# The softmax norm of the last two blocks placed in the output loop, on one Trainium2 core

## The chip, the cores and the metric

The kernel runs on one core of a Trainium2 chip. A core has five engines that run side by side, each through its own list of instructions in order: TensorE (PE in the profile, with its weight loads as PEld), VectorE (DVE), ScalarE (ACT), GpSimd (POOL) and SyncE (SP), which here issues nearly all DMAs. They wait for one another by semaphores. The metric is the device time of one execution in microseconds; less is better.

## The reference

A long convolution with a gate gives x, and x goes through a soft mixture of experts. Only the second part matters here:

```python
N, D, E, S_per_e, F = (45824, 128, 8, 4, 1024)
logits = x @ phi                                   # 45824 x 32
d = exp(logits - logits.max(0)); d /= d.sum(0) + 1e-09
slot_input = (d.T @ x).reshape(E, S_per_e, D)      # dispatch
slot_out[e] = relu(slot_input[e] @ w1[e]) @ w2[e]  # eight experts, four slots each
c = exp(logits - logits.max(1)); c /= c.sum(1) + 1e-09
out = c @ slot_out                                 # 45824 x 128
```

So there are two softmaxes of the same logits: down the tokens (d, for dispatch) and across the 32 slots (c, for the way back).

## The kernel before

The convolution fills the first 770 us and is not touched. The mixture works on the 45824 tokens as 358 tiles of 128, in 23 blocks of 16 tiles (the last, `L2` = 22, has 6; `L1` = 21 is the one before). Everything is written in program order by hand: `inorder` fixes the order of the instructions on each engine as the lines stand.

The main loop (L768) takes a block at a time. `logits` makes the block's logits in PSUM on PE; `slot_max`, `spread_max` and `running_max` keep the running maximum down the tokens; `exps` makes the exponentials for d on ACT; `scores` turns the logits on DVE so that a token's 32 lie in one partition; `softmax` subtracts a token's maximum (a reduce on DVE, then a subtraction on POOL, L661) and writes into `Cm`; `norm` makes the exponential of that on ACT (L667) and adds up the 32 by halves on POOL (L669 to L673) into `csum`; `turn_weights` turns the exponentials for d; `dispatch` multiplies them with the tokens on PE and `collect` adds the result to `acc`. `invert` (L700) makes the reciprocals of `csum` on DVE for a range of tiles, `scale` (L721) multiplies a block of `Cm` by them on POOL.

The tail (from L789) does the last two blocks, then the experts, then the outputs. `up` (PE, and a ReLU on ACT) makes 512 hidden values of four experts, `turn_hidden` turns them (PE, and four copies on DVE), `down` (64 matmuls of PE for four experts) sums into `po`. From `po` come, through one more matmul, the slot outputs `so` (L875), multiplied by `share` from `denominator`.

The output loop (L904) has 24 steps: `spread(m)` multiplies the turned weights of 16 tiles (4 and 12 in the first two steps) with `so` in four matmuls (L893), copies the four PSUM results into an SBUF buffer, two by DVE and two by ACT (L900), and issues one DMA of up to 1 MB to DRAM (L901). There are seven such buffers. The weights are turned by `turned` (four transposes of PE, a copy of DVE or ACT), five steps ahead of their use; the first five, `early(0)` to `early(4)`, are turned before the loop. From step 2 on, step m uses block m - 1 of `Cm`, so that `scale` must have run on it; `scale` of blocks 4 to 10, of 11 to 20, and of `L1` and `L2` stand in the tail, each group behind its `invert`.

Just ahead of the output loop the order is: `down(1)`, `norm` of `L1` and `L2`, `scale` of blocks 11 to 20, the copy of `po`, `so`, and then `invert(QL, QN)` and `scale` for `L1` and `L2`.

Of the kernel before, what the change touches and what calls it, by code (L numbers as in the profile page):

```python
# [34 lines left out]
QN = TOK // 128  # L35
# [462 lines left out]
class Moe:  # L498
# [71 lines left out]
    def run(self, ctx):  # L570
        _moe(ctx, self)


def _moe(ctx, mo):
# [3 lines left out]
    NBL = len(blocks)  # L578
# [54 lines left out]
    def running_max(i, rd):  # L633
        pm = pmt[:, 0:4]
        inorder(nc.tensor.matmul(pm, lhsT=reps, rhs=rd, start=True, stop=True))
        inorder(nc.vector.tensor_reduce(out=neg[:, i + 1 : i + 2], in_=pm, axis=AX.X, op=ALU.min))
# [12 lines left out]
    def scores(i):  # L649
        n = blocks[i][1]  # L650
        lts[i] = lt = ms.tile([128, NB, NSLOT], F32, tag="lt", name=f"lt_{i}")
        inorder(nc.vector.transpose(lt[:, :n].rearrange("p q s -> p (q s)"),
                            pls[i][:, :n].rearrange("p q t -> p (q t)")))
# [10 lines left out]
    def norm(i):  # L664
        q0, n = blocks[i]
        cv = Cm[:, q0 : q0 + n, :]
        inorder(nc.scalar.activation(cv, cv, AF.Exp))  # L667
        h = ms.tile([128, NB, NSLOT // 2], F32, tag="hs", name=f"hs_{i}")
        inorder(nc.gpsimd.tensor_tensor(out=h[:, :n], in0=cv[:, :, :16], in1=cv[:, :, 16:], op=ALU.add))  # L669
        for k in (8, 4, 2):  # L670
            inorder(nc.gpsimd.tensor_tensor(out=h[:, :n, :k], in0=h[:, :n, :k], in1=h[:, :n, k : 2 * k],  # L671
                                    op=ALU.add))
        inorder(nc.gpsimd.tensor_tensor(out=csum[:, q0 : q0 + n], in0=h[:, :n, 0], in1=h[:, :n, 1],  # L673
                                op=ALU.add))
# [9 lines left out]
    def dispatch(*ids):  # L684
        pa = pp.tile([128, 128], F32, tag="pa", name=f"pa_{ids[0]}")
        both = {i: (xq.pop(i), evs.pop(i)) for i in ids}
        parts = [(*both[i], k) for i in ids for k in range(blocks[i][1])]
        for m, (X, ev, k) in enumerate(parts):
            a = m % 4
            inorder(nc.tensor.matmul(pa[32 * a : 32 * a + 32, :], lhsT=ev[:, k, :], rhs=X[:, k, :],  # L690
                             start=(m < 4), stop=(m >= len(parts) - 4), tile_position=(0, 32 * a)))
        pas[ids[0]] = pa

    def collect(i):
        inorder(nc.vector.scalar_tensor_tensor(out=acc, in0=acc, scalar=fac[:, i : i + 1],
                                       in1=pas.pop(i), op0=ALU.mult, op1=ALU.add))

    QL = blocks[NBL - 2][0]

    def invert(q0, q1):  # L700
        inorder(nc.vector.tensor_scalar_add(csum[:, q0:q1], csum[:, q0:q1], 1e-9))
        inorder(nc.vector.reciprocal(csum[:, q0:q1], csum[:, q0:q1]))
# [4 lines left out]
    def den_sum():  # L707
        inorder(nc.scalar.activation(fin[:, : NBL - 2], neg[:, 1 : NBL - 1], AF.Exp, scale=-1.0,
                             bias=neg[:, NBL - 1 : NBL]))
        inorder(nc.vector.tensor_mul(sums, sums, fin))  # L710
        inorder(nc.vector.tensor_reduce(out=den, in_=sums, axis=AX.X, op=ALU.add))

    def denominator():
        ps = pmt[:, 4:8]
        inorder(nc.tensor.matmul(ps[:, 0:1], lhsT=reps, rhs=den, start=True, stop=True))
        rs = mp.tile([128, 1], F32, tag="rs", name="rs")
        inorder(nc.vector.tensor_scalar_add(rs, ps[:, 0:1], 1e-9))
        inorder(nc.vector.reciprocal(rs, rs))
        return rs

    def scale(i):  # L721
        q0, n = blocks[i]
        cv = Cm[:, q0 : q0 + n, :]
        inorder(nc.gpsimd.tensor_tensor(  # L724
            out=cv, in0=cv, op=ALU.mult,
            in1=csum[:, q0 : q0 + n].unsqueeze(2).to_broadcast([128, n, NSLOT])))
# [23 lines left out]
    def early(m):  # L750
        pt = pp.tile([128, 4, 128], F32, tag="pt", name=f"ct_{m}", bufs=4)
        turned(m, pt, True)

    EARLY = 5
# [12 lines left out]
    L1, L2 = NBL - 2, NBL - 1  # L767
# [26 lines left out]
    inorder(nc.vector.tensor_tensor(out=rm, in0=rm, in1=rm2, op=ALU.min))  # L794
    rd = spread_max(L1, rm)
    early(0)
    early(1)
    dispatch(L1 - 1)
    running_max(L1, rd)
    collect(L1 - 1)  # L800
    inorder(nc.gpsimd.memset(hT, 0.0))
    exps(L1)
    exps(L2, True)
    early(2)
    early(3)
    scores(L1)
    turn_weights(L1)
    scores(L2)
    turn_weights(L2)
    dispatch(L1, L2)  # L810
    collect(L1)
    den_sum()
    fetch(L2)
    pst = pp.tile([128, 512], F32, tag="pt", name="pst", bufs=4)
    inorder(nc.tensor.matmul(pst[:, :NSLOT], lhsT=acc, rhs=reps[:, :NSLOT], start=True, stop=True))
    siT = mp.tile([128, NSLOT], F32, tag="siT", name="siT")
    inorder(nc.vector.tensor_copy(out=siT, in_=pst[:, :NSLOT]))

    FJ = FF // 128
    hr = mo.obuf[0].rearrange("p (e h f) -> p e h f", e=2, h=2)  # L820
# [2 lines left out]
    def up(eg, hf):  # L823
        ph = pp.tile([128, 512], F32, tag="pl", name=f"ph_{eg}_{hf}", bufs=2)
        for a in range(4):
            inorder(nc.tensor.matmul(ph[32 * a : 32 * a + 32, :], lhsT=siT,
                                     rhs=w1t[:, 4 * eg + a, 512 * hf : 512 * hf + 512],
                                     start=True, stop=True, tile_position=(0, 32 * a)))
        inorder(nc.scalar.activation(hr[:, eg, hf], ph, AF.Relu))

    def turn_hidden(eg, hf):
        pt = pp.tile([128, 4, 4, NSLOT], F32, tag="pt", name=f"ht_{eg}_{hf}", bufs=4)
        for j in range(4):
            inorder(nc.tensor.transpose(pt[:, j].rearrange("p a s -> p (a s)"),
                                        hr[:, eg, hf, 128 * j : 128 * j + 128], ident))
        for a in range(4):
            s = 4 * (4 * eg + a)
            inorder(nc.vector.tensor_copy(out=hT[:, eg, 4 * hf : 4 * hf + 4, a, s : s + 4],
                                          in_=pt[:, :, a, s : s + 4]))

    def down(eg):
        for j in range(FJ):
            for a in range(4):
                inorder(nc.tensor.matmul(po[32 * a : 32 * a + 32, :], lhsT=hT[:, eg, j, a, :],
                                         rhs=w2t[4 * eg + a][:, j, :], start=(eg == 0 and j == 0),
                                         stop=(eg == 1 and j == FJ - 1), tile_position=(0, 32 * a)))
# [2 lines left out]
    up(0, 0)  # L849
    up(0, 1)  # L850
    share = denominator()
    invert(blocks[EB][0], QH)
    turn_hidden(0, 0)
    for i in range(EB, NBL // 2):
        scale(i)
    up(1, 0)
    turn_hidden(0, 1)
    up(1, 1)
    for i in (L1, L2):
        softmax(i)  # L860
    early(4)
    turn_hidden(1, 0)
    down(0)
    invert(QH, QL)
    turn_hidden(1, 1)
    down(1)
    for i in (L1, L2):
        norm(i)
    for i in range(NBL // 2, L1):
        scale(i)  # L870
    inorder(nc.vector.tensor_copy(out=sop, in_=po))
    pr = pp.tile([128, 128], F32, tag="pa", name="pr")
    inorder(nc.tensor.matmul(pr, lhsT=reps, rhs=sop, start=True, stop=True))
    so = mp.tile([128, 128], F32, tag="so", name="so")
    inorder(nc.vector.tensor_scalar_mul(so, pr, share))  # L875
    invert(QL, QN)
    scale(L1)
    scale(L2)
    pps.close()
    pc = ctx.enter_context(tc.tile_pool(name="pc", bufs=1, space=bass.MemoryType.PSUM,  # L880
                                        reuse_waits="tile"))
# [3 lines left out]
    def spread(m):  # L885
        q0, n = starts[m], sizes[m]
        ct = cts.pop(m)
        ot = obs[m % (XB + OB)].rearrange("p (k a t) -> p k a t", a=4, t=128)
        pos = []
        for a in range(min(4, n)):  # L890
            na = (n - a + 3) // 4
            po = pc.tile([128, 4, 128], F32, tag="po", name=f"pw_{m}_{a}", bufs=6)
            inorder(nc.tensor.matmul(po[:, :na].rearrange("p k t -> p (k t)"),  # L893
                             lhsT=so[NSLOT * a : NSLOT * a + NSLOT],
                             rhs=ct[NSLOT * a : NSLOT * a + NSLOT, :na].rearrange("p k t -> p (k t)"),
                             start=True, stop=True, tile_position=(NSLOT * a, 0)))
            pos.append((a, na, po))
        for a, na, po in pos:
            copy = nc.scalar.copy if a % 2 else nc.vector.tensor_copy
            inorder(copy(out=ot[:, :na, a], in_=po[:, :na]))  # L900
        nc.sync.dma_start(out=out[:, 128 * q0 : 128 * (q0 + n)],  # L901
                          in_=ot.rearrange("p k a t -> p (k a t)")[:, : 128 * n])

    for m in range(len(sizes)):  # L904
        spread(m)
        if m + EARLY < len(sizes):
            pt = pc.tile([128, 4, 128], F32, tag="ct", name=f"ct_{m + EARLY}", bufs=2)
            turned(m + EARLY, pt, False)
# [144 lines left out]
```

## Time and profile before

| what | us |
| --- | --- |
| median of 3 runs | 956.37 |
| lowest, highest | 954.85, 958.70 |
| the profiled execution | 951.48 |
| its span, first to last instruction | 949.7 |

| engine | busy us | share of the span |
| --- | --- | --- |
| PE | 902.1 | 95% |
| DVE | 735.0 | 77% |
| ACT | 445.6 | 47% |
| POOL | 382.0 | 40% |

Times in the profile are microseconds from the start of the span. The shares are an average over stages that have different limits; the stage in question is the last 85 us. There, "L701" names line 701 of the kernel as printed above, a tile is called by the program's name for it or for the memory that it lies in (`xreg` holds `acc`, `hT` and the output buffers, `E` holds `Cm` and `csum`, `pw` are the PSUM results of an output step, `ct` and `cs` the turned weights in PSUM and SBUF). In a timeline row stand start, duration, engine, line, operation, output and inputs, shape and count, and in brackets the idle time in front and what ended it.

### The profile page before, as it was taken

Reading aid. Unit: us, or ns where it says so; the run is one execution under the profiler, and the core shown is the slowest. Engines: PE = TensorE matmul, PEld = TensorE weight load, DVE = VectorE, ACT = ScalarE, POOL = GpSimd, SP = SyncE. Lnnn points to the kernel's source line nnn. Section 1 sums busy time; section 2 is a strip of 40 time slices with the busy share of each in tenths; the row PEclk is TensorE's granted clock in tenths of the full one; section 3 lists DMA queues with packets and bytes.
Section 4 is the critical chain, followed back from the end, with each engine's and each line's share of the span. In section 5 each row is a group of like instructions: output and inputs, shape, how many; then the busy total and the mean of one; then the engine's idle time right before and its main releaser. Section 6 shows DMA issues by size and latency. Waiting matters only on the chain.

```text
span 949.7 us, 33000 instructions
## 1 busy us (share of the span) xinstructions
PE 902.1 (95%) x14040; PEld 813.7 (86%) x14040; DVE 735.0 (77%) x1282; ACT 445.6 (47%) x964; POOL 382.0 (40%) x582
## 2 busy tenths in 40 slices
PE   6999999999999999999999999999999989998792
PEld 5999989999999999999999999999999977765341
DVE  7936769698889879879988997998694268876571
ACT  0655447415711741571174157117414458884461
POOL 5002760382076038207603820760282017876700
PEclk9999999999999999999999999999999999999895
DMA  8923985468745745774574577457247798764498
GB/s 258 397 73 123 338 283 174 125 175 248 225 122 183 235 124 173 245 232 121 176 242 123 174 242 223 131 174 245 82 128 241 229 356 270 262 222 109 201 416 373
DMA packets 104239, 201.18 MB, mean 212 GB/s; under 512 B 14167, under 2 KB 65577, under 8 KB 100252
## 3 DMA queue, kind: packets, MB, share of 16 engines
q1 hardware_dynamic: 103806, 198.89, 64.4%
q8 instruction: 111, 1.82, 0.8%
q14 instruction: 36, 0.29, 0.1%
q10 hardware_dynamic: 254, 0.11, 0.0%
q0 software_dynamic: 32, 0.07, 0.0%
HBM read 139.12 MB, written 59.90 MB: 210 GB/s over the span
## 4 chain that ended last, share of the span: by engine, by line
PE 80%; POOL 7%; DMA 4%; DVE 3%; issue 2%; ACT 2%; DVEq 0%; ACTq 0%; SPq 0%
PE p L296 22%; PE p L279 19%; PE p L331 17%; PE p L138 10%; PE f L160 3%; PE f L170 2%; PE pw L893 2%; POOL hs L671 2%; POOL E L661 2%; PE fl L181 2%; DMA out_dram<-xreg 2%; DMA hs<-E 2%; POOL hs L669 1%; POOL E L724 1%; PE ct L738 1%
## 5 line engine op out<-in xcount | busy, mean ns | idle before, releaser
L287 POOL TENSOR_TENSOR T<-m 111x256 f32<-111x256 f32 (+1 forms) x200 | 147.8, 739 | 420.2 <-DVE m L282 420.2
L282 DVE TENSOR_TENSOR m<-p,T 111x1024 f32<-111x1024 f32 (+1 forms) x175 | 200.1, 1207 | 23.9 <-PE p L279 22.9
L296 PE MATMUL p<-tab,T 111*99 111x112 f32 x2048 | 210.5, 261 | 2.6 <-DVE E L356 1.6
L296 PEld LDWEIGHTS p<-tab,T 111*99 111x99 f32 x2048 | 200.2, 170 | 10.2 <-issue 2.7
L279 PE MATMUL p<-T,W 128*111 128x128 f32 x1584 | 194.7, 278 | 0.0
L279 PEld LDWEIGHTS p<-T,W 128*111 128x111 f32 x1584 | 183.0, 173 | 7.3
L340 ACT ACTIVATE vc<-p 128x416 f32<-128x416 f32 x112 | 51.9, 515 | 284.1 <-DVE p L345 192.5
L331 PE MATMUL p<-tab,E 99*64 99x104 f32 x3584 | 172.2, 253 | 2.2 <-ACT E L302 1.1
L331 PEld LDWEIGHTS p<-tab,E 99*64 99x64 f32 x3584 | 161.4, 136 | 10.0 <-issue 1.8
L302 ACT ACTIVATE E<-p 99x448 f32<-99x448 f32 x256 | 130.6, 575 | 82.1 <-PE p L296 82.1
L288 POOL TENSOR_TENSOR T<-m 111x256 f32<-111x256 f32 (+1 forms) x200 | 146.3, 731 | 0.0
L150 ACT ACTIVATE T<-p 128x396 f32<-128x396 f32 x240 | 102.3, 530 | 5.6 <-PE p L138 5.5
L138 PE MATMUL p<-tab1x,x 53*64 53x99 f32 x3776 | 95.7, 248 | 2.3 <-DVE m L282 1.6
L138 PEld LDWEIGHTS p<-tab1x,x 53*64 53x64 f32 x3776 | 84.1, 132 | 9.2 <-DVE m L282 1.8
L345 DVE TENSOR_TENSOR p<-p,vc 128x832 f32<-128x832 f32 x56 | 57.4, 1026 | 14.5 <-ACT vc L340 14.5
L560 ACT ACTIVATE xreg<-pt 128x512 f32<-128x512 f32 x90 | 48.0, 601 | 4.9 <-PE pt L559 3.0
L229 DVE TENSOR_TENSOR x<-x,T 128x448 f32<-128x448 f32 x55 | 34.1, 620 | 18.5 <-DMA x<-in_xf_dram 11.9
L353 DVE TENSOR_TENSOR E<-p,E 128x824 f32<-128x824 f32 x46 | 46.8, 1016 | 1.6
L559 PE MATMUL pt<-ident,xreg 128*128 128x128 f32 x358 | 47.5, 278 | 0.0
L661 POOL TENSOR_TENSOR E<-lt,mx 128x512 f32<-128x512 f32 (+1 forms) x23 | 23.5, 1025 | 59.2 <-ACT et L642 59.2
L559 PEld LDWEIGHTS pt<-ident,xreg 128*128 128x128 f32 x358 | 40.1, 146 | 4.9 <-issue 2.8
L282 DVE TENSOR_TENSOR m<-p,E 111x1024 f32<-111x1024 f32 (+1 forms) x25 | 29.0, 1209 | 18.0 <-ACT E L186 15.4
(108 smaller groups left out, 972.0 us busy)
## 6 DMA issues: line engine op xcount, KB each, us to landing
x<-in_xf_dram SPq DMA_DIRECT2D x118, 256.0 KB, 4.2
out_dram<-xreg SPq DMA_DIRECT2D x21, 1024.0 KB, 12.7
E<-in_xi_dram SPq DMA_DIRECT2D x46, 412.0 KB, 3.9
scr<-E SPq DMA_DIRECT2D x84, 206.0 KB, 3.2
T<-in_vf_dram SPq DMA_DIRECT2D x65, 224.0 KB, 4.9
hs<-E SPq DMA_DIRECT2D x12, 1024.0 KB, 5.1
T<-hs SPq DMA_DIRECT2D x63, 176.0 KB, 3.7
mv<-in_vf_dram SPq DMA_DIRECT2D x42, 224.0 KB, 5.3
```

The source lines that it names most:

```text
L138: steady(g, nc.tensor.matmul(ps[h][RP * d : RP * d + RP, i, s, :], lhsT=sd[js, i, s, d, :], rhs=tab1x[js, J * (s + d) : J * (s + d + 1)], ...
L150: steady(g, nc.scalar.activation(dst, src, AF.Copy))
L279: steady(g, nc.tensor.matmul(ps[:, i].rearrange("p b c -> p (b c)"), lhsT=W[:, k0 + i, :], rhs=Tf[:, :, k0 + i, :], start=True, stop=True))
L282: inorder(nc.vector.tensor_mul(m[:, :n].rearrange("p k s e c i -> p k s (e c i)").rearrange("p k s (b c) -> p k s b c", c=CG), ps[:, :n].u ...
L287: inorder(nc.gpsimd.tensor_tensor(out=Ty[:, 0], in0=m[:, :n, 0, 0], in1=m[:, :n, 1, 1], op=ALU.subtract))
L288: inorder(nc.gpsimd.tensor_tensor(out=Ty[:, 1], in0=m[:, :n, 1, 0], in1=m[:, :n, 0, 1], op=ALU.add))
L296: inorder(nc.tensor.matmul(pk[:, i, 2 * s : 2 * s + 2, :].rearrange("p q r -> p (q r)"), lhsT=T[0:N1, s, 2 * k + i, u // 2, :, u % 2], rhs ...
L302: inorder(nc.scalar.activation(E[:J, :, :, c : c + 2].rearrange("p r q c -> p q r c"), ps[:, k, : 8 * R].rearrange("p (i q r) -> p q r i", ...
L331: inorder(nc.tensor.matmul(pv[RP * h : RP * h + RP, 2 * k + i, w, :], lhsT=E[:J, r, 2 - 2 * w + s, :], rhs=tab4[:, s, o : o + NJ], start=( ...
L340: inorder(nc.scalar.activation(vc[:, w], pv[:, :, 0, :], AF.Copy, scale=2.0 * w - 1.0))
L345: inorder(nc.vector.tensor_tensor(out=pw, in0=pw[:, 1:2].to_broadcast([128, 2, 4, NJ]), in1=vc, op=ALU.add))
L559: inorder(nc.tensor.transpose(pt[:, j, :], self.xt[i][:, k + j, :], self.ident))
```

## The change

- `norm(L1)` and `norm(L2)` move from behind `down(1)` into the output loop, behind `spread(4)`; `invert(QL, QN)` and the two `scale` of `L1` and `L2` move behind `spread(8)`. The ten `scale` of blocks 11 to 20 now stand behind `so`, but POOL, which does nothing between, meets them in the order subtractions of `softmax`, ten `scale`, sums of `norm`.
- `scores(L1)` and `scores(L2)` (the turned logits) move ahead of `exps`; `early(1)` to `early(4)` come in one row behind `exps`; `den_sum` moves behind the copy of `siT`.
- The experts' stage: `turn_hidden(0, 0)` comes ahead of `up(1, 0)` and both first turns ahead of `invert(blocks[EB][0], QH)`; `turn_hidden(1, 0)` comes ahead of the two `softmax`; `down(0)` is done in two halves with `turn_hidden(1, 1)` between, and `invert(QH, QL)` behind that.

No instruction is added or taken away.

```diff
     early(0)
-    early(1)
     dispatch(L1 - 1)
+    scores(L1)
     running_max(L1, rd)
     collect(L1 - 1)
+    scores(L2)
     inorder(nc.gpsimd.memset(hT, 0.0))
     exps(L1)
     exps(L2, True)
-    early(2)
-    early(3)
-    scores(L1)
+    for m in range(1, EARLY):
+        early(m)
     turn_weights(L1)
-    scores(L2)
     turn_weights(L2)
     dispatch(L1, L2)
     collect(L1)
-    den_sum()
     fetch(L2)
...
     inorder(nc.vector.tensor_copy(out=siT, in_=pst[:, :NSLOT]))
+    den_sum()
...
-    def down(eg):
-        for j in range(FJ):
+    def down(eg, j0=0, j1=FJ):
+        for j in range(j0, j1):
...
     share = denominator()
+    turn_hidden(0, 0)
+    up(1, 0)
+    turn_hidden(0, 1)
     invert(blocks[EB][0], QH)
-    turn_hidden(0, 0)
     for i in range(EB, NBL // 2):
         scale(i)
-    up(1, 0)
-    turn_hidden(0, 1)
     up(1, 1)
+    turn_hidden(1, 0)
     for i in (L1, L2):
         softmax(i)
-    early(4)
-    turn_hidden(1, 0)
-    down(0)
+    down(0, 0, FJ // 2)
+    turn_hidden(1, 1)
+    down(0, FJ // 2)
     invert(QH, QL)
-    turn_hidden(1, 1)
     down(1)
-    for i in (L1, L2):
-        norm(i)
-    for i in range(NBL // 2, L1):
-        scale(i)
     inorder(nc.vector.tensor_copy(out=sop, in_=po))
...
     inorder(nc.vector.tensor_scalar_mul(so, pr, share))
-    invert(QL, QN)
-    scale(L1)
-    scale(L2)
+    for i in range(NBL // 2, L1):
+        scale(i)
...
     for m in range(len(sizes)):
         spread(m)
+        if m == 4:
+            for i in (L1, L2):
+                norm(i)
+        elif m == 8:
+            invert(QL, QN)
+            scale(L1)
+            scale(L2)
         if m + EARLY < len(sizes):
```

## The prediction

> **What bounds the kernel now.** I read the chain of waits first, for the tail from the last dispatch on, then the windows over the output loop, and then the timeline between them. The chain, columns start, duration, engine, tile, line:
>
> ```profile
> 872.05 7.15 POOL E L724 x7
> ...
> 879.20 1.01 POOL E L661
> ...
> 884.59 0.21 POOL E L673
> 884.83 1.01 DVE E L701
> ...
> 886.07 0.24 DVE xreg L900
> ...
> 917.75 15.47 DMA out_dram<-xreg
> ```
>
> From 872 to 885 the chain lies on POOL: seven `scale`, then the two `softmax` subtractions, then both `norm`. Then DVE's `invert(QL, QN)` (L701), and only behind it DVE's first copy of an output (L900, 886.07). At the end it is the output DMAs. The windows (columns: window, length, busy of PE, PEld, DVE, ACT, POOL, granted clock, DMA share, GB/s) say how much of the loop is theirs:
>
> ```profile
> 887.00:887.50 0.50, 0.50 (x4) 0.00 (x0) 0.50 (x2) 0.00 (x0) 0.50 (x1) 0.50 0.14 53
> ...
> 889.50:890.00 0.50, 0.50 (x6) 0.00 (x0) 0.00 (x0) 0.17 (x1) 0.50 (x2) 0.50 1.09 455
> ...
> 891.50:892.00 0.50, 0.50 (x7) 0.31 (x5) 0.50 (x2) 0.50 (x2) 0.50 (x2) 0.80 0.01 0
> ...
> 893.00:893.50 0.50, 0.50 (x8) 0.39 (x4) 0.44 (x1) 0.40 (x1) 0.50 (x1) 1.00 0.59 246
> ...
> 905.00:910.00 5.00, 5.00 (x38) 2.41 (x36) 4.26 (x8) 4.00 (x8) 0.00 (x0) 1.00 1.00 413
> ...
> 947.00:947.50 0.50, 0.00 (x0) 0.00 (x0) 0.00 (x0) 0.00 (x0) 0.00 (x0) 0.50 0.20 78
> ```
>
> The first output moves from about 887.4, the second from 889.5, both done by 891.5, and then nothing moves until the third starts at about 893.2. From there the DMA engines are full to about 947.0: 53.8 us for 23.46 MB (128 x 45824 x 4 bytes) less the first two outputs (4 and 12 tiles of 64 KB, 0.26 and 0.79 MB), 22.41 MB, or 0.417 MB/us. The span ends 2.7 us behind. So the end is set by **when the third output can follow the second without a gap**; what follows costs bytes over rate, whatever the engines do, as long as they stay ahead.
>
> **Before the loop, part by part.** What stands on the path to `so` in the timeline:
>
> ```profile
> 862.16 0.22 DVE L629 SCALAR_TENSOR_TENSOR rd<-neg,rm,pmt 128x4 f32<-128x4 f32 x1
> ...
> 862.86 0.16 DVE L636 TENSOR_REDUCE neg<-pmt 128x1 f32<-128x4 f32 x1 [0.48 <-PE pmt L635]
> ...
> 863.20 0.70 ACT L642 ACTIVATE et<-pl,neg 128x512 f32<-128x512 f32 x1
> ...
> 864.09 0.72 DVE L652 STREAM_TRANSPOSE lt<-pl 128x512 f32<-128x512 f32 x1 [0.82 <-ACT et L642]
> ...
> 864.73 0.67 DVE L680 STREAM_TRANSPOSE ev<-et 128x512 f32<-128x512 f32 x1
> ...
> 865.55 1.50 PE L690 MATMUL pa<-xreg,ev 128*32 128x128 f32 x44 [1.80 <-DVE ev L680]
> ...
> 871.12 0.85 DVE L702 RECIPROCAL E<-E 128x112 f32<-128x112 f32 x1
> ...
> 873.58 0.66 PE L738 MATMUL ct<-ident,E 128*128 128x128 f32 x4
> ...
> 875.04 0.23 DVE L701 TENSOR_SCALAR E<-E 128x160 f32<-128x160 f32 x1
> ...
> 875.31 1.15 DVE L702 RECIPROCAL E<-E 128x160 f32<-128x160 f32 x1
> ...
> 877.07 1.96 PE L844 MATMUL pso<-xreg 128*32 128x128 f32 x64
> ...
> 879.97 0.35 DVE L875 TENSOR_SCALAR so<-pr,rs 128x128 f32<-128x128 f32 x1 [0.58 <-PE pr L873]
> ```
>
> *Turned logits first.* `scores(L1)` now stands 0.82 us behind the exponentials on DVE, and `turn_weights(L1)` behind it. Moved up, it runs at 862.4 to 863.1 while DVE had nothing to do but wait for the maximum; it pushes that maximum (862.86, 0.16) by 0.25 us, and the exponentials by as much. `turn_weights` then needs them alone: from 864.2 instead of 864.73, and dispatch from about 865.05, **0.5 us earlier**. Above, the gain could be 0.72 (the whole transpose); below, nothing, if the later maximum eats it.
>
> *early(1) to early(4)* are 15 transposes together; at 0.66 per four 2.5 us of PE, between the maximum (862.8) and the dispatch (865.05), where PE waits 1.80 today. That hides nearly all of them; if not, up to 0.3 is lost. Their ACT copies (about 2.1 us behind the exponentials) are through at 867, before the first `up` has ended and ACT is needed. In return early(4), 0.66 of PE at 873.58, leaves the `down` stretch. `den_sum` behind `siT` costs nothing: `denominator` needs it two microseconds later.
>
> *The FFN order.* `turn_hidden(0, 0)` and `(0, 1)` no longer wait on DVE for `invert(blocks[EB][0], QH)`, 0.85 us with its reciprocal alone; their copies are ready near 871.0 and 872.6. PE's own work, with 0.5 us less in front, 0.66 less for early(4), and `down(0)` in two halves around the last turn, ends `down(1)` at about 878.3 against 879.03: of the 1.16 I leave 0.4 to turns that now follow their ReLU or copy closely and wait for it. DVE has `invert(QH, QL)` (1.15 and 0.23) in front of the copy of `po`; it starts after the last turn's copies, 875.9, and is through near 877.3, one microsecond ahead of its need. So `so` comes **0.7 us earlier**, at 879.6 instead of 880.32. Bounds: 1.3 (dispatch 0.7 and early(4) whole), and 0.4 later (a DVE instruction that is late).
>
> The price is POOL's: its first `scale` starts behind `turn_hidden(0, 1)`, 873.75 instead of 872.05, 1.7 us later. It is off the path now: the loop first needs block 4 (at 880), scaled at 874.8.
>
> **The head of the loop.** The rows that carry it:
>
> ```profile
> 879.16 1.50 POOL L661 TENSOR_TENSOR E<-lt,mx 128x512 f32<-128x512 f32 x2
> ...
> 880.94 0.73 POOL L669 TENSOR_TENSOR hs<-E 128x256 f32<-128x256 f32 x1 [0.27 <-ACT E L667]
> ...
> 881.03 0.41 ACT L900 COPY xreg<-pw 128x128 f32<-128x128 f32 x2
> ...
> 881.39 0.92 PE L893 MATMUL pw<-cs,so 32*128 32x384 f32 x4
> ...
> 884.75 11.57 POOL L724 TENSOR_TENSOR E<-E 128x512 f32<-128x512 f32 x12
> ...
> 884.83 1.00 DVE L701 TENSOR_SCALAR E<-E 128x22 f32<-128x22 f32 x1 [4.51 <-POOL E L673]
> ...
> 886.35 1.65 PE L893 MATMUL pw<-cs,so 32*128 32x384 f32 x4 [4.05 <-DVE xreg L900]
> ...
> 886.55 17.04 SPq L901 DMA_DIRECT2D out_dram<-xreg  x9
> ...
> 888.98 2.09 PE L893 MATMUL pw<-cs,so 32*128 32x512 f32 x8
> ...
> 895.45 1.14 PE L893 MATMUL pw<-cs,so 32*128 32x512 f32 x8
> ...
> 904.77 0.60 ACT L745 COPY cs<-ct 128x512 f32<-128x512 f32 x1
> ...
> 905.42 1.29 DVE L900 COPY xreg<-pw 128x512 f32<-128x512 f32 x2 [0.37 <-PE pw L893]
> ...
> 905.46 1.07 ACT L900 COPY xreg<-pw 128x512 f32<-128x512 f32 x2
> ...
> 906.63 0.68 DVE L745 COPY cs<-ct 128x512 f32<-128x512 f32 x1
> ...
> 908.97 1.29 DVE L900 COPY xreg<-pw 128x512 f32<-128x512 f32 x2 [0.37 <-PE pw L893]
> ```
>
> ACT copied its part of the first output at 881.03; DVE, behind the `invert`, at 886.07. Without it DVE copies beside ACT: **5.0 us gone**. With the 0.7, DVE and ACT are done at about 880.75 and the first DMA is issued at 880.8 instead of 886.55; data followed 0.9 us behind issue.
>
> The ramp shortens too. PE waited over 4 us there, its clock was granted at 0.50 (windows above), and the third output's matmuls took 2.09 us where 1.14 is usual. After the change PE waits for nothing so long. Then with durations from the quoted rows and 0.68 for DVE's ct copy, spread(1) is copied at 882.6, spread(2) at 884.0. The second output's data starts at 883.5 and takes 0.79/0.417 = 1.9 us, to 885.4; the third could start at 884.9. No gap: full from 885.4 with 22.41 MB left, against 893.2 today. That is **7.8 us** in all: 0.7 + 5.0 + 2.1 for the ramp. If the clock dips all the same, the ramp keeps its old shape, and the sum is 5.7.
>
> [...]
>
> **What moves into the loop.** `norm(L1)`, `norm(L2)` behind spread(4): two exponentials on ACT, about 1 us; per two outputs (3.55 us, from 905.42 to 908.97) ACT has four copies of 0.53 and one of 0.60, so it is caught up within two. What they need, POOL's subtractions, is done at 873.75 + 7.15 + 1.5 = 882.4, before spread(4) ends at about 887.6. POOL then has ten `scale` in front of the sums: to 882.4 + 10 x 1.02 (7.15 for seven) = 892.6, and the sums took 3.86 (880.94 to 884.80): **896.5**. `invert(QL, QN)` stands on DVE behind spread(8), copied near 884.0 + 6 x 1.78 = 894.7 (3.55 per two outputs). So DVE waits 1.8 us, plus 0.5 for the two instructions; behind it stand the copies of spread(9) and, through PSUM, PE. By then 0.26 + 0.79 + 7 x 1.05 = 8.4 MB are produced and about 5.3 sent: 3.1 MB, 7.4 us of transfers are waiting. Output 9, late by 2.3 us, still comes some 3 us before DMA runs dry. Cost: nothing. The last blocks are turned at output 17, far behind.
>
> **Rivals.** *The wait returns inside the loop, and costs part.* If POOL ends its sums over 3 us later than 896.5, DMA runs dry, and each further microsecond is lost. For it: POOL starts 1.7 us later and everything piles on it. Against: twelve `scale` took 11.57 us beside DVE's copies of just this loop. With 4.8 us beyond the margin the gain is 3.0: 953.4.
>
> *Head without ramp.* The loop starts early but its first outputs come as slowly as today, because the clock or the order of PSUM buffers holds it: 5.0 to 5.7, 951 us. Against: the second output's matmuls at full clock took 0.92, not 1.65.
>
> *The change doesn't move the end*, if the transfers are slower when started earlier: 956.4. Against: 413 GB/s in the middle, full share, with all engines busy.
>
> *Slower:* the same place, spread(8), with POOL twice as slow. For the whole 7.8 to be eaten, the sums must end after 896.5 + 3.2 + 7.8 = 907.5, and the ten `scale` take 21 us instead of 10.2, 2.1 each. There is one lock-like row that makes this thinkable: L701 on 22 columns took 1.00, from 884.83 to the end of POOL's first `scale`, where 160 columns took 0.23. DVE waited for POOL there, though, not POOL for DVE. [...]
>
> **How the numbers follow.** The profiled execution took 951.48 us (span 949.7), the three runs 954.85 to 958.7, median 956.37; 4.9 us lie between, not seen in the profile. I take the gain off the median: 956.4 - 7.8 = **948.6**. Chances: forecast, gain 5.5 to 10 us, 0.62; head without ramp 0.13; wait in the loop 0.13; no move 0.07; slower 0.05. A measurement of this kernel tells 0.5%, 4.8 us, from no change. So faster 0.75, same 0.20, slower 0.05. The range 944.8 to 953.0 goes from the largest gain (10, and the runs' own spread) to the first two rivals.
>
> **What would show it.** In the new profile: `turn_weights(L1)` right behind the exponentials and dispatch near 865.0; `so` at 879.6; first output issued near 880.8, not 886.5; granted clock 1.00 through the head; DMA full from 883.5 to 939.2 without a gap; a DVE wait of about 2 us for POOL at L701 near 895, with DMA still full beside it. Wrong would be a DMA share under 0.9 between 895 and 905, a `scale` of over 1.5 us, or `so` not earlier than 880.3.

## The result and the profile after

| | before | after |
| --- | --- | --- |
| median of 6 runs, us | 955.89 | 945.38 |
| lowest, highest | 954.00, 958.70 | 942.44, 947.20 |
| profiled execution | 951.48 | 946.41 |
| its span | 949.7 | 944.6 |

The changed kernel takes 0.9896 of the time, 95% interval 0.9873 to 0.992: between 7.6 and 12.1 us less. Forecast were 948.6 us and a gain of 7.8.

The two profiled executions differ by 5.1 us only, and a reader must see why before comparing rows. The change begins behind the exponential of block `L1 - 1` on ACT (L667), the last instruction of the tail that both kernels have at the same point of the same work. From the timelines, before and after:

```profile
862.14 0.63 ACT L667 ACTIVATE E<-E 128x512 f32<-128x512 f32 x1 [1.77 <-POOL E L661]
```

```profile
865.36 0.63 ACT L667 ACTIVATE E<-E 128x512 f32<-128x512 f32 x1 [1.78 <-POOL E L661]
```

Before this **mark** the executions are 3.2 us apart, in code that is the same but for `early(1)`: its turns stand on PE about 1.6 us ahead of the mark in the kernel before, and behind it in the changed one. The mark itself waits for POOL in both (1.77 and 1.78 us). The profile of before is one that was early. From the mark to the end of the span it is 949.7 - 862.14 = 87.6 us before and 944.6 - 865.36 = 79.2 after: **8.3 us less**. I count from the mark from here on.

The chain of waits after the change (start, duration, engine, tile, line):

```profile
876.60 7.16 POOL E L724 x7
883.76 1.47 POOL E L661 x2
885.23 10.06 POOL E L724 x10
...
898.91 0.21 POOL E L673
899.12 0.02 issue
899.15 0.19 DVE E L701
...
915.63 12.56 DMA out_dram<-xreg
```

It still runs through POOL and through the invert (L701), which seems to say that nothing was gained. It only says where it was followed back to: the last copies waited for the buffer of the DMA issued at 915.63, and that issue goes back to the copies behind the invert. That DMA had been full all the while does not show in it. What has changed stands in the timeline of the loop's head:

```profile
881.92 0.35 DVE L870 TENSOR_SCALAR so<-pr,rs 128x128 f32<-128x128 f32 x1 [0.58 <-PE pr L868]
...
882.92 0.49 DVE L894 COPY xreg<-pw 128x128 f32<-128x128 f32 x2 [0.64 <-PE pw L887]
882.95 0.43 ACT L894 COPY xreg<-pw 128x128 f32<-128x128 f32 x2 [6.24 <-PE pw L887]
...
883.47 19.76 SPq L895 DMA_DIRECT2D out_dram<-xreg  x11
...
884.79 1.24 PE L887 MATMUL pw<-cs,so 32*128 32x512 f32 x8
...
899.15 0.18 DVE L701 TENSOR_SCALAR E<-E 128x22 f32<-128x22 f32 x1 [1.26 <-POOL E L673]
```

DVE copies the first output in the same moment as ACT. The first DMA is issued 18.1 us behind the mark, not 24.4. The third output's matmuls take 1.24 us, not 2.09. DVE still waits for POOL's sums, 1.26 us instead of 4.51, at a place where DMA has work. The windows (granted clock, DMA share and GB/s in the last three columns):

```profile
884.25:884.50 0.25, 0.25 (x7) 0.25 (x4) 0.20 (x1) 0.16 (x1) 0.25 (x1) 1.00 0.63 246
...
885.50:886.00 0.50, 0.50 (x7) 0.04 (x1) 0.05 (x1) 0.19 (x1) 0.50 (x1) 1.00 0.00 0
886.00:887.00 1.00, 1.00 (x10) 0.83 (x12) 1.00 (x2) 0.96 (x2) 1.00 (x2) 1.00 0.81 338
...
895.00:900.00 5.00, 5.00 (x32) 2.26 (x31) 3.30 (x7) 4.03 (x8) 3.76 (x12) 1.00 1.01 411
900.00:905.00 5.00, 4.27 (x18) 1.53 (x16) 3.36 (x6) 1.23 (x3) 1.24 (x2) 0.67 1.01 419
...
941.50:942.00 0.50, 0.00 (x0) 0.00 (x0) 0.00 (x0) 0.00 (x0) 0.00 (x0) 0.50 0.71 281
```

DMA is full from about 886.1, the second output, to 941.9. In 900 to 905, behind DVE's late copies, PE's clock drops, to 0.67 on average, and DMA does not notice: 419 GB/s.

### The profile page after: what moved, and what is told of

Same layout as the page of the kernel before. It is cut to its first block, busy times and chain, and to the rows that moved or that the text cites. A ratio compares the mean times of both kernels' runs of the same rounds, so it can differ in the third digit from the quotient of the medians.

```text
span 944.6 us, 32994 instructions
## 1 busy us (share of the span) xinstructions
PE 900.0 (95%) x14040; PEld 813.9 (86%) x14040; DVE 734.7 (78%) x1282; ACT 445.3 (47%) x964; POOL 381.8 (40%) x582
```

## The experiments

Each kernel has a profile of its own, and for each I give the mark, the time from the mark to the end of the span, and the ratio to the kernel before, with its interval.

| kernel | mark | mark to end | ratio |
| --- | --- | --- | --- |
| before | 862.14 | 87.6 | 1 |
| after | 865.36 | 79.2 | 0.9896 (0.9873 to 0.9920) |
| again | 866.58 | 79.1 | 0.9907 (0.9877 to 0.9938) |
| loop_only | 863.09 | 80.5 | 0.9921 (0.9892 to 0.9950) |
| front_only | 865.64 | 88.8 | 0.9997 (0.9977 to 1.0017) |
| wait_early | 864.47 | 92.0 | 1.0029 (1.0011 to 1.0046) |
| warm | 865.77 | 87.3 | 0.9980 (0.9961 to 0.9998) |
| warm_short | 863.95 | 85.2 | 0.9980 (0.9964 to 0.9996) |
| pool_plus4 | 866.83 | 81.9 | 0.9944 (0.9924 to 0.9964) |
| pool_plus10 | 867.72 | 90.0 | 1.0027 (1.0004 to 1.0051) |
| pool_plus10_late | 864.88 | 79.8 | 0.9902 (0.9865 to 0.9939) |
| turn_later | 864.56 | 79.1 | 0.9914 (0.9892 to 0.9936) |
| ffn_back | 864.18 | 79.0 | 0.9893 (0.9860 to 0.9926) |

**again**, the changed kernel unaltered.

> The changed kernel once more, beside new runs of the kernel before. Theory (the gain is 1.3 us of earlier slot outputs, 5.0 us of the wait taken out, and some 2 us of a ramp without a gap, 8.2 us when both profiles are laid on the same instruction, the exponential of block L1-1): ratio about 0.9914 (8.2 us), and in the new profile the DMA ends again about 77 us behind that instruction (84.9 in the kernel before). Rival (about 2 us more are gained somewhere ahead of the tail, since the medians differ by 10.5): ratio 0.989 again, and the instruction that serves as the mark comes earlier than in the kernel before.

From the mark it takes the same as the first time, within 0.12 us, while the marks are 1.2 us apart. The ratio is 0.9907. The rival gets no support from the marks: those of the kernels with the new order in front lie between 864.2 and 867.7, no earlier than those with the old one, 862.1 to 865.8.

**loop_only**, the kernel before with the loop's part alone:

```diff
-    for i in (L1, L2):
-        norm(i)
-    for i in range(NBL // 2, L1):
-        scale(i)
     inorder(nc.vector.tensor_copy(out=sop, in_=po))
...
-    invert(QL, QN)
-    scale(L1)
-    scale(L2)
+    for i in range(NBL // 2, L1):
+        scale(i)
...
         spread(m)
+        if m == 4:
+            for i in (L1, L2):
+                norm(i)
+        elif m == 8:
+            invert(QL, QN)
+            scale(L1)
+            scale(L2)
```

> The kernel before with nothing changed but the place of the norms, of the last invert and of the scales (in and ahead of the output loop, as in the changed kernel). Theory: the wait and the ramp are this part, so 6.5 to 7 us of the 8.2 remain, 949 us, ratio 0.9930; slot outputs 17.8 us behind the mark as before, first output issued at about 19.2, POOL's sums end 1.3 us earlier than in the changed kernel, so that DVE hardly waits in the loop. Rival (the order ahead of the loop brings the gain): under 3 us, ratio over 0.997.

7.1 us of the 8.3 are here. From the timeline of this kernel:

```profile
880.92 0.35 DVE L871 TENSOR_SCALAR so<-pr,rs 128x128 f32<-128x128 f32 x1 [0.58 <-PE pr L869]
...
896.79 0.17 DVE L701 TENSOR_SCALAR E<-E 128x22 f32<-128x22 f32 x1
```

The slot outputs come 17.8 us behind the mark as before, and DVE does not wait at the invert at all, since POOL began its scales earlier than in the changed kernel.

**front_only**, the other half: the changed kernel's order up to the slot outputs, but norms, scales and invert ahead of the loop, where the kernel before has them. The edit is against the changed kernel.

```diff
+    for i in (L1, L2):
+        norm(i)
+    for i in range(NBL // 2, L1):
+        scale(i)
     inorder(nc.vector.tensor_copy(out=sop, in_=po))
...
+    invert(QL, QN)
+    scale(L1)
+    scale(L2)
...
-        if m == 4:
-            for i in (L1, L2):
-                norm(i)
-        elif m == 8:
-            invert(QL, QN)
-            scale(L1)
-            scale(L2)
```

> The changed kernel's order up to the slot outputs, with the norms, the last invert and the scales where the kernel before has them, ahead of the loop. Theory: slot outputs 1.3 us earlier, but POOL starts its scales 1.3 us later and DVE's first copy still waits for POOL's sums, so the first output is issued 1.3 us LATER than before: ratio 1.0014, 957 us, within what can be told from no change and certainly no gain. Rival (the earlier slot outputs are a gain of their own): 1.3 us or more faster, ratio under 0.9986.

```profile
882.21 0.35 DVE L874 TENSOR_SCALAR so<-pr,rs 128x128 f32<-128x128 f32 x1 [0.58 <-PE pr L872]
889.68 1.00 DVE L701 TENSOR_SCALAR E<-E 128x22 f32<-128x22 f32 x1 [7.12 <-POOL E L673]
```

`so` is 1.3 us earlier from the mark (16.6), but DVE now waits 7.12 us for POOL instead of 4.51, and from the mark the kernel takes 1.2 us **more** than before; the ratio cannot be told from 1. The earlier `so` is worth something only with the loop's part.

**wait_early**, the changed kernel with the wait at the wrong place:

```diff
-        if m == 4:
+        if m == 1:
             for i in (L1, L2):
                 norm(i)
-        elif m == 8:
+        elif m == 2:
```

> The changed kernel with the norms behind spread(1) and the last invert and two scales behind spread(2), in place of 4 and 8. POOL's work keeps its order. Theory (the wait for POOL's sums is still there and is only covered by outputs that wait for DMA; at output 2 there are none): DVE waits about 11 us at the invert, DMA runs dry for about 12 us, the third DMA moves at about 12 us later than in the changed kernel; 4 us slower than the kernel before, 960 us, ratio 1.004. Rival (it is enough that the invert stands behind the first outputs): as the changed kernel, ratio 0.990.

```profile
898.23 0.18 DVE L701 TENSOR_SCALAR E<-E 128x22 f32<-128x22 f32 x1 [11.88 <-POOL E L673]
```

```profile
886.00:890.00 4.00, 2.86 (x16) 1.11 (x11) 0.35 (x1) 2.69 (x6) 4.00 (x5) 1.00 0.94 385
890.00:892.00 2.00, 0.00 (x0) 0.00 (x0) 0.00 (x0) 0.00 (x0) 2.00 (x3) 0.68 0.00 0
892.00:896.00 4.00, 0.00 (x0) 0.00 (x0) 0.00 (x0) 0.00 (x0) 3.84 (x6) 0.50 0.00 0
896.00:900.00 4.00, 0.08 (x2) 0.08 (x2) 1.74 (x5) 0.00 (x0) 2.92 (x9) 0.50 0.00 0
```

The same instructions in the same order on POOL, and the kernel is slower than before, by 4.5 us from the mark (by the ratio, 1.1 to 4.4). DMA has sent its three outputs by 890 and then has nothing for over ten microseconds. So the place in the loop is the change; "into the loop" alone would have been a loss.

**pool_plus4, pool_plus10 and pool_plus10_late** measure the cover. In the changed kernel POOL gets extra work ahead of the last sums, 9 memsets in the first and 22 in the other two; in the last alone the invert moves to step 12. The edit shows both, with the first one's count:

```diff
     obs = mo.obuf + mo.xbuf
+    junk = mp.tile([128, 512], F32, tag="junk", name="junk")
...
         if m == 4:
+            for k in range(9):
+                inorder(nc.gpsimd.memset(junk, 0.0))
             for i in (L1, L2):
                 norm(i)
-        elif m == 8:
+        elif m == 12:
```

> The changed kernel with nine extra memsets of 128x512 on POOL (about 4 us) ahead of the sums of the last two norms. Theory (DVE's wait in the loop is covered by outputs that queue for DMA; by the changed kernel's trace output 9 is copied at 902.8 and DMA would run dry about 1.9 us after that): DVE waits about 5.3 us at the invert, DMA is without work for about 2 us, mark to end 81.3 instead of 79.2. Rival (no cover at all: each us of POOL is lost): 83.2. Rival (the cover is larger than 4 us): 79.2.

> As pool_plus4 with 22 memsets, about 10 us. Theory: the same margin of 1.9 us, so 8 us are lost and the whole gain with them: mark to end 87.3, no better than the kernel before (87.6). Rival (no cover): 89.2. Rival (a large cover): under 83.

> As pool_plus10, with the last invert and two scales behind spread(12) instead of spread(8). Theory (the place sets the cover: by then more outputs wait for DMA and POOL's sums are nearly done): DVE waits 4 to 5 us at the invert, DMA stays full, mark to end 79.2 to 79.7, all of the loss is gone though POOL's work is the same. Rival (the extra POOL work costs by itself, wherever the invert stands): 85 or more.

The memsets were longer than I had assumed. From the timelines of pool_plus4 and pool_plus10:

```profile
896.71 5.17 POOL L903 MEMSET junk<- 128x512 f32 x9
...
905.73 0.18 DVE L701 TENSOR_SCALAR E<-E 128x22 f32<-128x22 f32 x1 [6.37 <-POOL E L673]
```

```profile
897.60 12.73 POOL L903 MEMSET junk<- 128x512 f32 x22
...
914.18 0.18 DVE L701 TENSOR_SCALAR E<-E 128x22 f32<-128x22 f32 x1 [13.93 <-POOL E L673]
```

5.17 us on POOL cost 2.7 (81.9 against 79.2), 12.73 cost 10.8: all but 2.5 and 1.9 us is lost, and from the first to the second 7.6 us more of POOL cost 8.1. The loss is not one gap of DMA but two. In pool_plus4:

```profile
907.00:908.00 1.00, 0.58 (x2) 0.50 (x4) 1.00 (x3) 0.00 (x0) 0.82 (x2) 0.50 0.24 98
908.00:909.00 1.00, 1.00 (x4) 0.00 (x0) 0.56 (x1) 0.00 (x0) 0.00 (x0) 0.50 0.33 139
...
914.00:915.00 1.00, 1.00 (x9) 0.13 (x6) 0.00 (x0) 0.28 (x1) 0.00 (x0) 0.89 0.33 139
```

The first gap is the wait. At 413 GB/s it leaves out 1.4 us of transfers, and DVE waits 5.1 us longer than in the changed kernel: the wait alone has a cover of 3.7 us (in pool_plus10, 9.1 us left out and 12.7 waited longer: 3.6). The second gap, 0.85 us from 913 to 915 (1.4 in pool_plus10, with 342 and 367 GB/s in the halves of 920 to 930), comes behind outputs that PE made at the clock of 0.50 that the wait had left it, until about 914.2.

The expected 81.3 and 87.3 become 82.5 and 90.0 with these durations; 81.9 and 90.0 were measured. That they fit is partly luck: the output copied at 902.8 in the changed kernel is output 10, counted from 0 as the steps are. Output 9 was issued at 901.45, so that its margin is 3.3 us and not 1.9, and the clock, which the expectation leaves out, took about the difference back. With the invert four steps later the 12.73 us cost 0.6:

```profile
911.36 0.18 DVE L701 TENSOR_SCALAR E<-E 128x22 f32<-128x22 f32 x1 [6.85 <-POOL E L673]
```

DVE waits 6.85 us, and DMA stays at 401 GB/s or more in each of the windows of a microsecond from 905 to 918. It dips only later, to 380 GB/s in 920 to 925, behind outputs that PE made at a clock of 0.50 (910.2 to 920.4).

**warm and warm_short** ask what the ramp of 2 us was. In the kernel before, PE gets work to do while DVE waits, 26 matmuls in the first and 14 in the second:

```diff
             turned(m + EARLY, pt, False)
+        if m == 0:
+            fill = pc.tile([128, 4, 128], F32, tag="ct", name="fill", bufs=2)
+            for k in range(26):
+                inorder(nc.tensor.matmul(fill[:, k % 4, :], lhsT=reps, rhs=ident, start=True, stop=True))
```

> The kernel before with its wait left as it is, and 26 extra matmuls on TensorE (about 3.8 us, written to a PSUM tile that nobody reads) behind the first turned tile in the output loop, so that TensorE works while DVE waits for POOL. Theory (the ramp of 2 us is the clock that falls to 0.50 while TensorE waits): clock stays 1.00, the third output's eight matmuls take 1.1 to 1.3 us instead of 2.09, its DMA follows the second without a gap, and the time from the mark (the exponential of block L1-1) to the end of the span falls by about 2.2 us, from 87.6 to 85.4; ratio 0.998. Rival (the ramp is the order of copies behind a late DVE, the clock only goes with it): 87.6, no change.

> As warm, with 14 extra matmuls in place of 26. In warm they took 5.97 us instead of 3.8, so that they ended 1.2 us after DVE was free and held back the second output; 14 take about 3.2 us and end before. Theory (the ramp is the clock): second output's copies done 0.5 us earlier than in the kernel before, third output follows without a gap, mark to end 85.4 instead of 87.56; ratio 0.9975. Rival (the ramp is the order behind a late DVE): 87.5.

In *warm* the 26 matmuls ran for 5.97 us, over DVE's return, and from the mark it gained only 0.2. But this execution was late before the loop: DVE waited 2.43 us for the dispatch (L695), not 1.17, which puts the dispatch at 2.77 us instead of 1.50, and `so` came 19.1 us behind the mark, not 17.8. From DVE's invert (L701) to the end it took 63.4 us against 64.9 before: 1.5 us less, so that it speaks for the clock too. In *warm_short*, where `so` comes at 17.8:

```profile
883.10 3.29 PE L912 MATMUL fill<-ident,reps 128*128 128x128 f32 x28
886.32 0.91 PE L893 MATMUL pw<-cs,so 32*128 32x384 f32 x4
888.16 0.92 PE L893 MATMUL pw<-cs,so 32*128 32x384 f32 x4 [0.92 <-DVE xreg L900]
889.04 0.63 PE L738 MATMUL ct<-ident,E 128*128 128x128 f32 x4
889.60 1.14 PE L893 MATMUL pw<-cs,so 32*128 32x512 f32 x8
```

With the wait for POOL left as it is (4.51 us), the second half of the second output takes PE 0.92 us instead of 1.65 and the third output 1.14 instead of 2.09, the clock is 1.00 through the head of the loop, and the kernel is 2.4 us faster from the mark. That is the ramp: the slow start was the clock that PE had lost while it waited, not the order of the copies.

**turn_later** tries to close the last gap, between the first and second output (885.0 to 886.1 in the changed kernel):

```diff
-        if m + EARLY < len(sizes):
-            pt = pc.tile([128, 4, 128], F32, tag="ct", name=f"ct_{m + EARLY}", bufs=2)
-            turned(m + EARLY, pt, False)
+        t = m + EARLY - 1
+        if EARLY <= t < len(sizes):
+            pt = pc.tile([128, 4, 128], F32, tag="ct", name=f"ct_{t}", bufs=2)
+            turned(t, pt, False)
```

> The changed kernel with the turning inside the output loop one step later (step m turns the weights of step m + 4, none in step 0). In the changed kernel the first output's data is through at 885.0 and the second's starts at 886.1, because DVE copies a turned tile (0.69) and TensorE turns it (0.59) ahead of the second output. Theory (the end is set by when DMA becomes full): the gap falls from 1.1 to about 0.4, mark to end 78.5 instead of 79.2, ratio about 0.9906, a little under the changed kernel. Rival (a step less of lead in the turns makes PE wait for DVE later): 79.2 or more.

A miss: 79.1, no gain. The second output moved up, but then the third was late, and the gap stood in front of it:

```profile
886.50:887.00 0.50, 0.50 (x6) 0.14 (x2) 0.29 (x1) 0.45 (x2) 0.50 (x1) 1.00 0.52 197
887.00:887.50 0.50, 0.50 (x8) 0.33 (x7) 0.50 (x2) 0.50 (x2) 0.50 (x2) 1.00 0.62 262
```

The third output's data comes 22.6 us behind the mark, where in the changed kernel the second's transfer ends, 1.9 us after 886.1, at 22.7. What the second output gains the third does not: PE and DVE still have the same work to do before the third is ready, about 1.8 us for an output, and only from there on are they ahead of the transfers, which take 2.5 us for 1 MB at 413 GB/s.

**ffn_back** gives the experts' stage its old order, except that `early(4)` stays ahead of the dispatch:

```diff
+    invert(blocks[EB][0], QH)
     turn_hidden(0, 0)
+    for i in range(EB, NBL // 2):
+        scale(i)
     up(1, 0)
     turn_hidden(0, 1)
-    invert(blocks[EB][0], QH)
-    for i in range(EB, NBL // 2):
-        scale(i)
     up(1, 1)
-    turn_hidden(1, 0)
     for i in (L1, L2):
         softmax(i)
-    down(0, 0, FJ // 2)
-    turn_hidden(1, 1)
-    down(0, FJ // 2)
+    turn_hidden(1, 0)
+    down(0)
     invert(QH, QL)
+    turn_hidden(1, 1)
     down(1)
```

> The changed kernel with the experts' stage in the order of the kernel before (early(4) stays ahead of the dispatch, the turned logits stay ahead of the exponentials). Theory (of the 1.3 us that the slot outputs come earlier, 0.75 are there at the dispatch, the rest comes from the experts' stage): dispatch 2.7 us behind the mark as in the changed kernel, slot outputs about 17.1, mark to end 79.7. Rival (the experts' order gives nothing, all is in front): slot outputs 16.6, mark to end 79.2. Rival (it gives all): slot outputs 17.8, 80.4.

```profile
866.86 1.50 PE L690 MATMUL pa<-xreg,ev 128*32 128x128 f32 x44 [0.31 <-DVE ev L680]
...
880.75 0.35 DVE L869 TENSOR_SCALAR so<-pr,rs 128x128 f32<-128x128 f32 x1 [0.58 <-PE pr L867]
...
896.63 0.17 DVE L701 TENSOR_SCALAR E<-E 128x22 f32<-128x22 f32 x1
```

Here the first rival is right: dispatch 2.7 and `so` 16.6 us behind the mark, both as in the changed kernel. The new order of the experts gives nothing to `so`; it only holds POOL's scales back, and without it DVE does not wait at the last invert. With 79.0 from the mark this is as fast as the changed kernel (the ratios 0.9893 and 0.9896 can't be told apart) with less changed and more cover. No version was found that is faster than these two by more than the runs tell.

## Why the prediction was right

**What bounds the end.** Shown: wait_early and the three kernels with more POOL work move the end by what DMA idles. In wait_early about 12.7 us of transfers at 413 GB/s are left out (11.5, 0.8 and 0.3 in three gaps), and it ends 12.8 us later from the mark than the changed kernel. The full transfers behind the second output, 53.8 us before, take 53.9 in the changed kernel (888.0 to 941.9).

**The wait taken out, 5.0 us, and the ramp, 2.1 us.** The first output was issued 6.3 us earlier from the mark; 1.3 of that is `so`, so the wait was worth 5.0. The ramp gave the rest, 8.3 - 6.3 = 2.0. That the ramp is the clock is what warm_short showed, with 2.4 us.

**The slot outputs, 0.7 us.** The sign was right, the size was not: 1.3. The dispatch came 0.74 us earlier instead of 0.5, because the exponentials were not pushed at all (1.00 us behind the mark, 1.06 before). I had the maximum pushed by 0.25 us by the turned logits; it ended 0.90 us behind the mark and 0.88 before. And ACT, which in the kernel before still had the copy of early(1) in front, began 0.10 us behind the maximum instead of 0.18. In the experts' stage I counted 0.66 for early(4) and gave 0.4 back to turns that would wait; from the start of the dispatch to `so` it was 14.42 before and 13.89 after, 0.53 less, and ffn_back has the same 13.89 with the old order. So the order of turns and products that I took for a part of it was worth nothing. What is left is early(4), out of the way with its 0.66, and `den_sum`: of the 0.53 us, 0.09 are there when `up` starts (2.79 us behind the start of the dispatch, now 2.70). Neither was tried by itself. The rows from the timeline of the changed kernel:

```profile
865.89 1.83 PE L738 MATMUL ct<-ident,E 128*128 128x128 f32 x15
...
866.36 0.69 ACT L642 ACTIVATE et<-pl,neg 128x512 f32<-128x512 f32 x1 [0.22 <-DVE neg L636]
...
868.03 1.50 PE L690 MATMUL pa<-xreg,ev 128*32 128x128 f32 x44 [0.31 <-DVE ev L680]
```

The 15 early transposes were hidden as forecast: 1.83 us, in a time in which PE still waited 0.31 for the turned weights.

**POOL's later start.** I took 1.7 us and it was 1.3 (11.2 us behind the mark instead of 9.9). With the loop's part it costs nothing: ffn_back, where POOL starts 9.1 us behind the mark, ends at 79.0, the changed kernel at 79.2. Without the loop's part it costs all of it, as front_only showed.

**DVE's wait in the loop.** Forecast 1.8 us and a cover of some 3 beyond it; measured 1.26, and by the first gaps of pool_plus4 and pool_plus10 a cover of 3.7 and 3.6 beyond that. So the sum for output 9 was right. What it left out is the clock: I let the outputs behind the wait come at full clock, and the second gaps, 0.85 and 1.4 us, are the price when they don't (0.50), so that only 2.5 and 1.9 us of POOL's work were free in all. In the changed kernel the clock falls there too, at 901.7, but by then output 9 had been issued, and DMA stayed full. The rival that would have made the kernel slower needed the sums about 11 us later than forecast; pool_plus10, with 12.7 us more on POOL, shows such a kernel, 0.27% slower than before. Nothing in POOL's work slowed it here: ten scales took 10.1 us beside the loop's copies.

**The level.** The prediction took the profile's gain, 7.8, off the median, and the tail gave 8.3. The medians lie 10.5 us apart in the first comparison and 9.7 in the second; by the ratios it is 9.9 and 8.9. So the gain came out at the upper edge of the 5.5 to 10 that I gave it, and 945.4 is 3.2 us under the forecast, of which the tail explains 0.5. 8.3 us are 0.9913, inside both intervals. Whether the rest is anything but the spread of what runs ahead of the mark stays open; the profiles show no gain there. The 4.9 us between the profiled execution of before and its median are of the size of that spread: the thirteen marks lie up to 5.6 us apart, and that of before, 862.14, is the earliest.

## What to carry to other kernels

An engine's wait in a loop that a full DMA queue ends costs nothing while enough outputs are queued for DMA, and its whole length where none are (here 1.26 us behind step 8 cost nothing, 11.88 us behind step 2 cost 12.8): work out the cover, bytes produced less bytes sent, at the step where the wait is put, and leave room for outputs that come at a lower clock behind it (0.50 in pool_plus4, with a second gap of 0.85 us). A wait at the head of such a loop can cost more than its own length: here DVE's 4.51 us cost 5.0, and the first outputs, which PE then made at a clock of 0.50, another 2.0. And time gained on one input of a join is a gain only if the other input is not later: front_only had the slot outputs 1.3 us earlier and was 1.2 us slower from the mark.

## What was not expected of the hardware

PE's granted clock fell after much less than the wait of before, in which PE had stood still for 4.05 us. In the changed kernel PE had only a short gap behind the invert in the loop, yet it ran at a clock of 0.50 afterwards:

```profile
898.99 1.13 PE L887 MATMUL pw<-cs,so 32*128 32x512 f32 x4
...
900.84 1.28 PE L887 MATMUL pw<-cs,so 32*128 32x512 f32 x4 [0.73 <-DVE xreg L894]
```

```profile
901.00:901.50 0.50, 0.50 (x4) 0.14 (x4) 0.50 (x2) 0.00 (x0) 0.24 (x1) 1.00 1.02 426
901.50:902.00 0.50, 0.50 (x4) 0.00 (x0) 0.48 (x1) 0.00 (x0) 0.00 (x0) 0.68 0.90 377
...
905.00:905.50 0.50, 0.50 (x7) 0.38 (x4) 0.29 (x1) 0.25 (x1) 0.00 (x0) 0.90 0.86 360
```

There is a gap of 0.73 us at 900, and then 0.50 from about 901.7 to 905.1, some 3.4 us; the kernel run again shows the same from 903.5 to 907.0. In as long a stretch ahead of the fall PE was busy for 2.7 (2.68 of 3.41, and 2.69 of 3.42 in the second run), where the loop otherwise keeps it busy all the time (5.00 of 5.00 us from 895 to 900). I had expected no fall here, since PE waits for nothing as long as before. Ahead of it stood a stretch that was thin, not idle; that the stretch was its cause is my reading, and no run tries it. The profile of before had shown such a fall already: its clock falls to 0.50 at about 925.8, where PE had been busy for 2.30 of the 3.25 us from 922.50 to 925.75 and its longest wait was 0.74.

The add of the invert (L701, DVE, SBUF to SBUF) looks as if POOL's instruction in flight holds it up. On 22 columns it took 0.17 to 0.18 us with POOL idle (after, loop_only) and 1.00 where one of POOL's scales, about 1.02 us, had begun 0.08 us before (before, front_only). In ffn_back, beside the scales, 160 columns took 0.61:

```profile
873.27 7.09 POOL L724 TENSOR_TENSOR E<-E 128x512 f32<-128x512 f32 x7 [4.36 <-DVE xreg L837]
...
875.83 0.61 DVE L701 TENSOR_SCALAR E<-E 128x160 f32<-128x160 f32 x1
```

Three scales from 873.27 end at about 876.3, and the add ends at 876.4. Where the add of 160 columns began within 0.1 us of a scale's end, it took 0.23 (at 875.04 before and 878.60 after; by 1.02 us for a scale they end at about 875.1 and 878.6). The rows agree with such a hold; why there should be one, and whether DVE holds POOL up in the same way, no run here shows.

The matmuls that *warm* added cost 0.23 us each (5.97 for 26, with 52 records), where turning a tile of the same 128x128 takes 0.12 to 0.17 (1.83 for 15 in the changed kernel, 0.66 for four). Why is open.
